# Moving a second batch from dense masked attention to gathered key blocks in a fused attention and feed-forward kernel

## The chip, the cores and the metric

The kernel runs on one core of one Trainium2 chip. The metric is device time in microseconds of one execution. A core has PE (TensorE, the matrix engine, with its weight loads shown apart as PEld), ACT (ScalarE), DVE (VectorE), POOL (GpSimd) and SP (SyncE), which here only issues transfers. Sixteen DMA engines serve all queues.

## The reference

```python
def _attn_ref(q, k, v, sampled_blocks):          # q, k, v: (4, 8, 768, 64)
    scores = scale * np.matmul(q, k.transpose(0, 1, 3, 2))
    # blocks of 32; 24 blocks; window of one block on each side; first and last block: rows and columns
    mask = np.abs(blk_i - blk_j) <= window
    mask = mask | (blk_i == 0) | (blk_j == 0) | (blk_i == n_blocks - 1) | (blk_j == n_blocks - 1)
    for qb in range(n_blocks):
        for kb in sampled_blocks[qb]:            # 3 sampled blocks for each query block
            mask[qb * block:(qb + 1) * block, kb * block:(kb + 1) * block] = True
    attn = softmax(np.where(mask, scores, -1e9))
    return np.matmul(attn, v)

def _moe_ref(x, w_in, w_out):                    # 3072 tokens, 512 -> 2048 -> 512
    r = np.maximum(x @ w_in, 0.0)
    return (r * r) @ w_out
```

The attention output of each batch, with its heads side by side, is the input of the feed-forward part. The sampled blocks come as an input, so which key blocks a query block needs is known only when the kernel runs.

## The kernel before, in words

Matmuls run in bfloat16. A unit `u` is a pair of heads of one batch; each of the four batches has four units. The feed-forward part runs on tiles T of 256 tokens, three per batch: four `hidden` groups (each four PE parts), `relu`, `square`, then `output` in eight parts, `out_copy` and `store`.

There are two ways of attention, and `SB` tells how many batches go the first way.

*Dense and masked* (batches 0 and 1 before). `scores` multiplies 256 queries with two chunks of 128 keys, `exps` takes the exponential of 1024 columns on ACT, `masks` multiplies it on DVE with a 0/1 mask `MK` (line 365), and `values` or `values_full` multiplies with V. A column of ones beside V gives the sum for `normalize`. For batch 0's first 256 queries the mask is added inside PSUM instead. `MASKED` lists the column ranges for which mask tiles are made; they lie in the buffers `VG` that the sparse batches use later.

*Gathered blocks* (batches 2 and 3 before). A visit `v` takes two pairs of query blocks, `g`. For each `g` the keys are gathered into `KG`: `k_gather` copies the window, the first and last block and the six sampled blocks out of the transposed keys of all four units, on POOL or DVE, at addresses read from registers (lines 590 to 596). V goes to DRAM by `v_store` once all four units' values are cast; `v_gather` fetches the sampled rows from there, by an indirect transfer on POOL (line 575) or by six transfers on SP, and `v_window` fetches the window and the edges. Then come `s_scores` (line 204), `s_exps` (621), `s_masks` with the small mask `MKS` (628), `s_values` (651), `s_normalize` and `s_transp`. Visit 0 has beside its one pair the query blocks at the two ends, which see all keys.

The tables for this, block numbers and `MKS`, are made by `table_load` (SP), `table_places` (POOL), `table_slots` (some 25 small DVE instructions, lines 480 to 507), `table_spread` (PE), `table_rows` and `table_masks` (DVE).

`prepare` makes each unit's loads. From unit 4 on they wait for a gate: `loads_gate` is a tiny transfer on SP that waits for a block of weights. Loads are cast to bfloat16 (`cast_qk`, `cast_v`), and q and k are transposed by DMA (`transp_dma`). Raw loads have few buffers, three for q, two each for k and v:

```python
            g = gate[GATES[min(u - HP, len(GATES) - 1)]]
...
            x = T_(transp_dma, u, w, deps=[c] + old_s, put=[qc])
```

`QKT` and `VB` hold two batches: a unit's transposes wait for the scores of the unit eight before it. A dense unit needs its own keys and queries only; a visit needs those of all four units:

```python
            kc[g] = T_(k_gather, b, v, g, get=[] if kc else [kb], deps=[ev[u][1, 0] for u in us] + ...
```

Everything is a numbered task, and `PROGRAM` is the order, written out as words: engine letter, task number and, after a slash, the PSUM buffer. Each engine runs its words strictly in this order. For loads of units that go the dense way the rows of q and k are read in runs of 1536 bytes, for the others in runs of 512 (`qn`, `kn`).

Of the kernel before, what the change touches and what calls it, by code (L numbers as in the profile page):

```python
# [13 lines left out]
BF = mybir.dt.bfloat16  # L14
# [5 lines left out]
P = 128  # L20
# [5 lines left out]
def kernel(  # L26
# [12 lines left out]
    B, H, S, D = q.shape  # L39
# [3 lines left out]
    d_model = H * D  # L43
# [17 lines left out]
    SB, VR, KG_BUFS, VG_BUFS = 2, D + 2, 2, 3  # L61
# [16 lines left out]
    MASKED = ((256, 512), (512, 768), (0, 256))  # L78
# [60 lines left out]
    RT, YS = many("r", R_BUFS, [P, TWM], F32), many("ys", YS_BUFS, [P, 2 * d_model], F32)  # L139
# [310 lines left out]
    dup, low = consts.tile([GR, SL - 4], F32, name="dup"), {}  # L450
# [22 lines left out]
    def table_slots(e):  # L473
        tmp = RT[tb["tmp"][0].at]
# [4 lines left out]
        low[0] = RT[tb["tmp"][1].at][0:D].bitcast(BF)[:, 0:5 * P].rearrange("g (s c) -> g s c", c=P)  # L479
# [301 lines left out]
    def T_(f, *args, **kw):  # L781
        return Task((lambda e: f(*args, e)), **kw)
# [146 lines left out]
    tb, mk_claims, mk_buf = {}, [], {}  # L929
# [34 lines left out]
    for T in TILES:  # L964
# [36 lines left out]
        V109 V153 V207 V332 V18 V19 V20 V28 V42 V53 V294 V29 A32 V35 P30/0 P36/1 P0/2 P33/3 V31 V37 A1 P11/0 V34 P100/1 G46 A101  # L1001
        P47/0 P104/2 V43 A105 P44/3 P102/1 V45 V57 V48 P58/2 A103 V54 P111/3 V59 P55/0 P113/2 A112 V56 P115/1 V41 P4/0 A114 G64 P9/0
        P125/3 P2/0 A116 G52 P106/2 V3 V67 A126 P5/0 P123/1 V107 G74 P65/0 A124 P108 V66 P121/3 V110 G63 P68/0 A122 P82/2 V69 P84/1
        V83 P131/0 A85 P135/2 A132 G49 P86/3 P117/1 V87 G60 A136 P88/0 P10/3 V118 P133/3 G73 A89 P61/2 P119 G38 A134 V62 P12/0 G75
        V120 P90/0 P168/2 P15/1 V91 A169 P39/1 P174/3 G78 V40 P127/0 G76 A175 P137/1 V128 G70 P144/2 V138 P129 P147/3 A145 V130 P139
        V176 P71/0 A148 V140 P171/2 V170 P781/1 P782 V72 A172 V146 P92/3 P187/0 P783 V93 A188 P784 V173 P50/2 P181/3 A785 P177/0
        V189 V51 A182 P141/1 G786 V178 P774/2 P775 A142 V149 P184/3 P179 P776 G79 G22 V180 A185 P94/1 P777 V143 P155/0 A95 V778 G787
        P150/3 A156 P158/1 V151 P161/2 A159 P788/0 V183 P152 P789 S80 V186 A154 P215/1 A162 P790 V157 P14/3 P791 V160 A216 P98/3
        P190/2 V163 A99 P212/1 S251 V792 A780 P164/3 S252 A213 V191 P795/0 G793 A779 V165 P796 S81 P209/1 G794 P192 P166 P797 V167
        V193 P798 A210 P824/3 V217 V214 S259 S260 V383 G77 P825 A799 P197/2 P194/1 P826 A198 G801 P827 P818/0 A195 V828 P819 G254  # L1010
        P226/2 A800 P820 S255 V196 A227 P200/1 P812/3 V264 P813 A201 V211 S267 P243/2 P821 V256 S265 P814 A244 V228 P218/1 P815 V199
        A822 P219 P802/2 A816 V220 S257 V202 P240/0 P221 P803 A241 V262 S261 P96/3 P804 A222 V97 A817 P237/0 V242 P223/1 P203/3 A238
        S268 V245 P805 S263 V272 A224 P229/0 P204 P806 A230 G266 S275 S276 P286/1 V225 A823 P807 S273 V231 A287 P808 V205 P232/0
        A829 V270 P206 P289/1 S271 P233 V239 V208 P809 A290 V234 V288 P296/3 S253 A810 P246/1 V291 S437 P235 P247 V236 A297 P299/2
        V248 P830/0 P831 A300 V280 P302/3 V278 P832 A303 P249 S279 P283/2 V250 P833 V298 A284 P852/1 V834 V434 P314/3 S277 P853 A315
        S281 P846/2 V304 P847 A835 V285 P311/0 P854 V258 P855 A312 V301 P848 S269 P849 V316 A856 P292/3 S21 V313 P864/0 A850 P293
        P305/1 G282 V295 P865 A857 P308/2 G851 S454 P306 S436 A309 P866 V307 P353/3 P867 A354 P326/1 V868 P858/2 G439 P859 A327
        P320/3 P860 V274 A321 P323/0 S438 V310 P836/1 S444 A324 V355 S460 P861 V322 P347/3 S445 P837 V496 A862 V328 V325 G441 P317/0
        A348 P350/2 P318 P838 S811 V319 A351 V349 P329/3 A869 P334/0 V352 P330 P839 V331 A335 V23 P356/2 G443 A863 P340/3 P840 S333
        A341 P841 P362/0 P357 G447 P842 A363 P337/3 P843 S452 A338 G459 S442 P870/0 G449 A844 P359/3 P871 S446 A360 V345 V342 V358  # L1020
        S440 V339 P374/1 P872 A375 V336 P365/2 S450 P377/3 V361 P873 A366 V364 P343/1 S462 A378 V367 P371/2 P344 S845 P874 A372 S448
        V346 V376 P368/3 P398/1 V373 P369 A399 P875 V379 S461 V370 P380/2 V470 S453 P401/1 P381 A402 P385/3 V382 P876 V400 A386 S384
        P391/2 P16/1 P877 V451 A392 V403 P404/1 P886/3 V878 A405 P887 P388/2 P425/0 A389 V406 P24/1 P888 V27 V25 A426 P889 P880/2
        A890 P881 G463 P428/0 P882 A429 G467 P883 V427 V26 S613 P407/3 G465 S631 A884 P408 S468 S469 A891 G455 S464 V396 V409 P926/0
# [64 lines left out]
```

## Time and profile before

| | |
|---|---|
| median of 3 runs | 260.05 us (257.1 to 262.1) |
| profiled execution | 257.99 us |
| its span, first to last instruction | 256.1 us |
| mean granted TensorE clock | 0.991 |
| PE, ACT, DVE, POOL busy | 95%, 72%, 65%, 38% of the span |
| DMA | 47.08 MB, mean 184 GB/s |

The span is what the engines' rows cover; the profiled time is 1.9 us longer. In a row of the windows the first number is the length of the stretch, then come busy microseconds and instruction counts (x) of each engine, the granted clock, the mean busy share of the DMA engines and GB/s. The DMA share adds queues that overlap, so it can pass 1. In a row of the timeline stand the start, the length, the engine, the line, the operation, output and inputs, the shape and the count. In a row of groups stand count, busy time in all, mean nanoseconds of one, and the idle time ahead of them with what ended it.

### The profile page before, as it was taken

To read this page: it belongs to the slowest core of one execution; us is meant where nothing else is said; L and a number is where in the kernel's file an instruction comes from. 1 tells how busy PE (TensorE), PEld (TensorE's weight loads), DVE (VectorE), ACT (ScalarE), POOL (GpSimd) and SP (SyncE) were. 2 spreads that over 40 slices of the span, in tenths; PEclk is the share of its full clock that TensorE was granted. 3 is DMA by queue.
4 is the path that set the end of the run, shared out by engine and by line. 5 is a ranking of instruction groups with operands and counts; after the bars stand their busy time and mean duration, and the time that the engine had idled before them with its cause. 6 is when DMAs were issued, how large, how long until landed. Compare 5 with 4: busy or idle time off the path is not lost.

```text
span 256.1 us, 12046 instructions
## 1 busy us (share of the span) xinstructions
PE 243.1 (95%) x5265; PEld 182.3 (71%) x5265; DVE 166.4 (65%) x386; ACT 184.5 (72%) x217; POOL 98.0 (38%) x199
## 2 busy tenths in 40 slices
PE   7699999999999998999999987999999999999995
PEld 4577889679865677886757854766975775776774
DVE  7578997789789889865446925646466478543300
ACT  3899999999998798965867662778697646325241
POOL 2175533010544033566737951062428406151030
PEclk9999999999999999999999997999999999999999
DMA  6999999999799998999999998951525554343022
GB/s 182 368 266 196 196 241 217 270 209 254 211 316 200 206 196 256 127 276 187 289 241 165 213 197 204 303 148 34 153 50 87 150 159 112 96 119 91 3 84 84
DMA packets 63540, 47.08 MB, mean 184 GB/s; under 512 B 31487, under 2 KB 58496, under 8 KB 63488
## 3 DMA queue, kind: packets, MB, share of 16 engines
q1 hardware_dynamic: 58352, 37.61, 66.7%
q0 software_dynamic: 4448, 8.25, 15.7%
q8 instruction: 41, 0.67, 1.1%
q10 hardware_dynamic: 688, 0.46, 0.6%
q14 instruction: 11, 0.09, 0.1%
HBM read 35.51 MB, written 7.91 MB: 170 GB/s over the span
## 4 chain that ended last, share of the span: by engine, by line
PE 88%; DMA 4%; DVE 2%; issue 1%; ACT 1%; another core or an unknown queue 1%; SPq 1%; DVEq 0%; ACTq 0%
PE X L204 80%; PE X L651 5%; DMA ks<-in_k_dram 2%; DMA xT<-XS 2%; PE X L396 2%; ACT pT L358 1%; PE X L306 1%; DVE ys L124 1%; DVE qc L124 0%; SPq L170 0%; PE X L425 0%; DVE QKT L124 0%; DVE pT L365 0%; DVE VB L124 0%
## 5 line engine op out<-in xcount | busy, mean ns | idle before, releaser
L204 PE MATMUL X<-xT,w_in_sb 64*128 64x256 bf16 x1536 | 99.8, 270 | 4.5 <-remote 2.5
L204 PE MATMUL X<-w_out_sb,g 64*128 64x512 bf16 (+3 forms) x960 | 95.8, 336 | 0.0
L204 PEld LDWEIGHTS <-w_in_sb 64*128 64x128 bf16 x1536 | 74.7, 94 | 16.6 <-remote 3.0
L358 ACT ACTIVATE pT<-X 128x1024 bf16<-128x1024 f32 x72 | 70.7, 1032 | 7.3 <-PE X L204 5.5
L621 ACT ACTIVATE pT<-X 128x768 bf16<-128x768 f32 (+1 forms) x56 | 41.7, 765 | 29.5 <-PE X L204 27.8
L204 PEld LDWEIGHTS <-g 64*128 64x128 bf16 x960 | 40.8, 95 | 26.7 <-issue 1.4
L716 ACT ACTIVATE g<-r 128x1024 bf16<-128x1024 f32 (+1 forms) x44 | 40.2, 929 | 11.8 <-DVE r L707 11.7
L707 DVE TENSOR_SCALAR r<-X 128x1024 f32<-128x1024 f32 x22 | 26.9, 1224 | 26.3 <-PE X L204 24.8
L365 DVE TENSOR_TENSOR pT<-pT,VG 128x1024 bf16<-128x1024 bf16 x60 | 41.0, 719 | 2.0 <-ACT pT L358 1.3
L718 POOL TENSOR_TENSOR g<-r 128x512 bf16<-128x512 f32 (+1 forms) x16 | 20.7, 1307 | 48.4 <-ACT r L705 24.8
L628 DVE TENSOR_TENSOR pT<-pT,MKS 128x768 bf16<-128x768 bf16 (+1 forms) x48 | 28.8, 631 | 13.1 <-ACT pT L621 12.7
L705 ACT ACTIVATE r<-X 128x1024 f32<-128x1024 f32 x26 | 27.3, 1063 | 9.7 <-PE X L204 8.1
L204 PE MATMUL X<-QKT 64*128 64x256 bf16 (+1 forms) x384 | 32.1, 250 | 0.7 <-issue 0.4
L575 POOL DMA_INDIRECT VG<-rows,idx x20 | 20.1, 1004 | 26.0 <-PE X L651 12.0
L204 PEld LDWEIGHTS <-QKT 64*128 64x128 bf16 x384 | 17.4, 95 | 6.4 <-issue 1.9
L204 PEld LDWEIGHTS <-pT 64*128 64x128 bf16 x768 | 15.5, 94 | 2.8 <-PE X L204 0.2
L124 POOL CAST VB<-vs 128x768 bf16<-128x768 f32 x10 | 8.5, 855 | 23.5 <-DMA vs<-in_v_dram 21.9
L204 PEld LDWEIGHTS <-KG 64*128 64x128 bf16 x528 | 13.9, 96 | 4.9 <-issue 1.0
L204 PE MATMUL X<-VB,pT 64*128 64x65 bf16 x768 | 17.2, 190 | 0.1
L124 POOL CAST qc<-ks 128x384 bf16<-128x384 f32 (+1 forms) x17 | 8.5, 530 | 21.0 <-DMA ks<-in_k_dram 16.0
L204 PE MATMUL X<-QKT,KG 64*128 64x64 bf16 x528 | 15.5, 191 | 0.3 <-issue 0.3
L596 POOL COPY KG<-QKT 128x64 int32 x72 | 14.8, 251 | 0.0
(104 smaller groups left out, 198.3 us busy)
## 6 DMA issues: line engine op xcount, KB each, us to landing
vs<-in_v_dram SPq DMA_DIRECT2D x14, 384.0 KB
ks<-in_k_dram SPq DMA_DIRECT2D x13, 384.0 KB
qs<-in_q_dram SPq DMA_DIRECT2D x12, 384.0 KB
out_dram<-ys SPq DMA_DIRECT2D x9, 512.0 KB
VG<-rows SPq DMA_DIRECT2D x20, 132.0 KB
w_in_sb<-in_moe_w_in_dram POOLq DMA_DIRECT2D x2, 1024.0 KB
w_out_sb<-in_moe_w_out_dram POOLq DMA_DIRECT2D x4, 512.0 KB, 11.0
rows<-VB SPq DMA_DIRECT2D x4, 396.0 KB
```

The costliest lines, as they stand in the source:

```text
L124: (V if e == "DVE" else G).tensor_copy(out=out, in_=in_)
L204: last = nc.tensor.matmul(out(r ^ crossed), lhsT(r ^ crossed, rows), rhs(r ^ crossed, rows), skip_group_check=True, **kw)
L358: A.activation(out=pT[:, :, 0:n], in_=stile.pop(a)[:, :, 0:n], func=AF.Exp, scale=scale)
L365: V.tensor_tensor(out=pT, in0=pT, in1=m[:, None].broadcast_to([P, 2, len(cs), w]), op=AOP.mult)
L575: G.indirect_dma_start(out=to[0:RS * HB], out_offset=None, in_=pairs, in_offset=bass.IndirectOffsetOnAxis(ap=idx[0:RS * HB, g - 1:g], axis=0))
L596: eng.tensor_copy(out=rows[:, :, :, r_ * w:(r_ + 1) * w], in_=src[:, :, :, bass.ds(at[r_] * w, w)])
L621: A.activation(out=pT[:, :, 0:n], in_=stile.pop((u, v, gs))[:, :, 0:n], func=AF.Exp, scale=scale)
L628: V.tensor_tensor(out=pT, in0=pT, in1=m[:, None].broadcast_to([P, 2, n]), op=AOP.mult)
L705: A.activation(out=to, in_=src, func=AF.Relu)
L707: V.tensor_scalar(out=to, in0=src, scalar1=0.0, scalar2=None, op0=AOP.max)
L716: A.activation(out=g, in_=r, func=AF.Square)
L718: (G if e == "POOL" else V).tensor_mul(out=g, in0=r, in1=r)
```

## The change

`SB` goes from 2 to 1, so batch 1 takes the gathered way: its loads are read in the layout of batches 2 and 3, its dense scores, masks and values go, and it gets `v_store`, `v_window`, `v_gather`, `k_gather` and six visits of its own. The mask tiles for columns 0 to 256 served batch 1 alone and go. `table_slots` works in one YS buffer rather than in two r buffers, and the tables are made in the first quarter of the program, since the first visit now comes before batch 0's feed-forward part is done. The numbers of the tasks and all orders are new.

```diff
-    SB, VR, KG_BUFS, VG_BUFS = 2, D + 2, 2, 3
+    SB, VR, KG_BUFS, VG_BUFS = 1, D + 2, 2, 3
...
-    MASKED = ((256, 512), (512, 768), (0, 256))
+    MASKED = ((256, 512), (512, 768))
...
     def table_slots(e):
-        tmp = RT[tb["tmp"][0].at]
+        tmp, spread_ = YS[tb["tmp"].at][:, 0:d_model], YS[tb["tmp"].at][:, d_model:2 * d_model]
...
-        low[0] = RT[tb["tmp"][1].at][0:D].bitcast(BF)[:, 0:5 * P].rearrange("g (s c) -> g s c", c=P)
+        low[0] = spread_[0:D].bitcast(BF)[:, 0:5 * P].rearrange("g (s c) -> g s c", c=P)
...
-    tmp = tb["tmp"] = [Buf("r"), Buf("r")]
-    tb["slots"] = T_(table_slots, deps=[t, p], get=tmp)
+    tmp = tb["tmp"] = Buf("ys")
+    tb["slots"] = T_(table_slots, deps=[t, p], get=[tmp])
...
-    t = T_(table_spread, hb, deps=[tb["slots"]], get=[hb], put=tmp)
+    t = T_(table_spread, hb, deps=[tb["slots"]], get=[hb], put=[tmp])
```

In the new `PROGRAM` the parts that the prediction speaks of stand like this. The order of the weight loads on POOL was blocks 0, 1, 4, 2, 5, 3 and is 0, 1, 4, 3, 2, 5. SP issues the first gate, unit 4's q, the tables and unit 4's v, the second gate, then k of 4 and 5, q of 7 and 6, v of 5, transposes of 4, and so on until both `v_store` of batch 1, in front of the last transposes of units 6 and 5. The tables' DVE work:

```text
before:  ... V331 A335 V23 P356/2 G443 A863 P340/3 P840 S333 A341 P841 P362/0 P357 ...
after:   ... V184 P159 P205/0 S246 P773 A160 V204 A206 P208/2 P774 P185 P775 A209 V22 P219/0 S80 A186 ...
```

(V23 before and V22 after are `table_slots`.) The three last parts of the output of tile (2, 0) stood ahead of the first visit of batch 3 on PE and stand behind it now; the other PE work behind that visit is the same.

More of the change, by code (lines that the diff above doesn't have):

```diff
@@ L1005 @@
[L1005 to L1012, printed above, removed]
@@ new lines @@
+        A942 P973 G982 V603 A577 P974 S582 P951 V975 P570/3 P965/0 S602 A571 V578 P966 G563 P573/2 P514/3 A574 G609 P967 V539 S592
+        G589 P952 S538 P968 P953 G587 S610 V515 S604 P567/2 P954 A568 V572 V575 S517 A969 V569 P551/3 P955 A976 G970 P959/2 P960
+        A552 P545/0 P956 A546 S600 G540 V553 P554/3 V957 A555 G619 S606 S588 P961 S542 P962 G541 P579/0 V559 A963 P548/3 V644
+        P1011/1 V580 A964 P999/2 P1000 G611 A597 P1005/0 P1001 A549 G648 P1002 P1012 V605 S614 A1003 V556 P632/3 P1006 S615 P1013
@@ L1057 @@
+        P1183 P1184 P1195 S1170 P1196 P1197 P1198 P1185 P1186 V1199 P1187 P1188 S1200 A1189 S1190
     """
```

97 lines of the change are left out of this document (49 added, 48 removed).

## The prediction

> **What bounds the kernel now.** I read the page's busy times and its chain first, then the windows by stage, then PE's timeline, then the DMA view by stretch.
>
> ```profile
> PE 243.1 (95%) x5265; PEld 182.3 (71%) x5265; DVE 166.4 (65%) x386; ACT 184.5 (72%) x217; POOL 98.0 (38%) x199
> PE 88%; DMA 4%; DVE 2%; issue 1%; ACT 1%; another core or an unknown queue 1%; SPq 1%; DVEq 0%; ACTq 0%
> ```
>
> By this PE bounds nearly everything. The windows (PE, PEld, DVE, ACT, POOL busy us, clock, DMA share, GB/s) say more:
>
> ```profile
> 10.00:37.00 27.00, 26.02 (x559) 21.75 (x556) 23.15 (x51) 26.16 (x32) 13.92 (x27) 1.00 1.12 243
> 37.00:64.00 27.00, 26.98 (x614) 22.58 (x611) 22.68 (x44) 26.41 (x30) 4.31 (x5) 1.00 1.11 234
> 64.00:97.00 33.00, 32.47 (x751) 22.82 (x743) 28.77 (x72) 30.23 (x33) 12.22 (x17) 1.00 1.08 222
> 97.00:120.00 23.00, 22.25 (x533) 18.23 (x534) 17.09 (x45) 17.98 (x23) 11.36 (x35) 1.00 1.13 218
> 120.00:143.00 23.00, 21.84 (x500) 16.12 (x495) 13.14 (x26) 15.83 (x19) 15.61 (x42) 1.00 1.13 220
> 143.00:166.00 23.00, 20.48 (x415) 14.82 (x410) 13.21 (x33) 12.74 (x15) 8.27 (x9) 0.93 1.12 235
> 166.00:180.00 14.00, 14.00 (x307) 9.47 (x302) 7.01 (x29) 11.44 (x15) 6.33 (x18) 1.00 0.38 95
> ```
>
> Two things besides PE are full. ACT works 97% of the time until 64 us. And the DMA share stands at 1.08 to 1.13 in every stretch until 166 us, then falls to 0.38: the DMA engines work without a break until the last batch is in, and only then does PE run alone. The chain shows what PE did around that point:
>
> ```profile
> 92.22 5.40 DMA xT<-XS
> ...
> 118.63 1.64 PE X L651 x67
> ...
> 152.51 2.47 another core or an unknown queue
> ...
> 179.28 1.64 PE X L651 x69
> ```
>
> The 1.64 us pieces are the first visits of batches 2 and 3 (`s_values` with v = 0). So batch 3's values were in by 166 plus the gather behind them, and PE wanted them at 179.3. A gather takes some 6 us from POOL's start to landing, by a row of the DMA view from 105 to 165 us:
>
> ```profile
> DMA  9199999999999999999929999999979939987989
> q1 hardware_dynamic: 19981, 10.76, 99.5%
> q0 software_dynamic: 704, 2.23, 13.8%
> VG<-rows,idx POOLq DMA_INDIRECT x11, 5.7
> ```
>
> So the data was ready at about 166 + 6 = 172, and DMA is only some 7 us behind PE as the bound. That is the slack on which this change must live.
>
> **The change: what PE saves.** Rows of PE's timeline; the step from one start to the next is what a task costs:
>
> ```profile
> 85.55 0.53 PE L204 MATMUL X<-VB,pT 64*128 64x65 bf16 x24
> 85.91 0.38 PE L204 MATMUL X<-QKT 64*128 64x256 bf16 x4
> 86.14 0.54 PE L204 MATMUL X<-VB,pT 64*128 64x65 bf16 x24
> 86.51 1.03 PE L204 MATMUL X<-w_out_sb,g 64*128 64x512 bf16 x8
> 87.38 0.53 PE L204 MATMUL X<-VB,pT 64*128 64x65 bf16 x24
> ...
> 207.50 0.95 PE L651 MATMUL X<-VG,pT 128*64 128x65 bf16 x48
> 208.39 0.35 PE L204 MATMUL X<-QKT,KG 64*128 64x64 bf16 x12
> 208.57 1.03 PE L204 MATMUL X<-w_out_sb,g 64*128 64x512 bf16 x8
> ```
>
> Dense batch 1 is 36 score tasks at 0.23 = 8.3 us and 24 half `values` at 0.365 = 8.8; three mask tiles for columns 0 to 256, six matmuls of the same width, add 0.3. Together 17.4 us. Sparse it is 24 score tasks of twelve matmuls at 0.18 and 4 of six at 0.09 = 4.7, five `s_values` at 0.89 and one at 1.64 = 6.1; together 10.8. **PE saves 6.6 us** of 256; skipping two thirds of the blocks saves little, because short matmuls cost more per column.
>
> **ACT, DVE, POOL.**
>
> ```profile
> L358 ACT ACTIVATE pT<-X 128x1024 bf16<-128x1024 f32 x72 | 70.7, 1032 | 7.3 <-PE X L204 5.5 <-ACT g L716 0.6 <-PE X L425 0.5
> L365 DVE TENSOR_TENSOR pT<-pT,VG 128x1024 bf16<-128x1024 bf16 x60 | 41.0, 719 | 2.0 <-ACT pT L358 1.3 <-ACT r L705 0.6
> L621 ACT ACTIVATE pT<-X 128x768 bf16<-128x768 f32 x48 | 38.0, 811 | 26.8 <-PE X L204 25.2 <-DVE KG L596 1.1
> L628 DVE TENSOR_TENSOR pT<-pT,MKS 128x768 bf16<-128x768 bf16 x40 | 25.6, 670 | 10.6 <-ACT pT L621 10.2 <-issue 0.4
> L596 POOL COPY KG<-QKT 128x64 int32 x72 | 14.8, 251 | 0.0
> L575 POOL DMA_INDIRECT VG<-rows,idx x20 | 20.1, 1004 | 26.0 <-PE X L651 12.0 <-DVE XS L411 7.0 <-issue 3.8
> ```
>
> ACT loses 36 x 1.03 = 37 us and gets 20 x 0.81 plus eight smaller, about 20: 17 us less. DVE loses 26 us of masks and gets 13 plus small ones plus five of the eleven key gathers: about even. POOL gets six key gathers (six copies of 0.25 and a longer one, about 2 each) and eleven issues of 1.0: 23 us more, on an engine idle 60% of the time. None of these is priced by itself: PE hid them, as its rows of 27.00 and 33.00 us show (98 to 100% busy).
>
> **The tables, moved from 75 us to about 40.** They are one piece of DVE work, between these rows:
>
> ```profile
> 74.46 0.20 DVE L480 COPY tab<-sb_r 1x72 int32<-1x72 int32 x1
> ...
> 80.54 0.16 DVE L507 TENSOR_TENSOR lane<-lane,half 128x1 f32<-128x1 f32 x1
> ```
>
> That is 6.2 us. In the new DVE order `table_slots` stands among the masks of batch 0's last columns, and behind it wait the masks of (1, 512) and (2, 512), for them ACT's exps when the eight pT buffers are full, and then PE. Between the words around it PE has only about 3.7 us of its own (five scores, two hidden parts, two output parts). In the old place it had over 6. I take 3 us of stall, bounds 0 and 6. The YS buffer that it borrows holds a v load of the start, cast long before, and the first output copy comes later: no cost.
>
> **Batch 1 must be whole.** Before, batch 1's first scores needed unit 4 alone; now `k_gather` needs the keys of all four units and `s_values` their values through DRAM. SP's and POOL's rows bound when they can start:
>
> ```profile
> 28.30 0.80 POOL L332 DMA_DIRECT2D w_out_sb<-in_moe_w_out_dram  x1
> ...
> 31.66 0.25 SPq L336 DMA_DIRECT2D scratch<-w_out_sb  x1
> 37.88 0.24 SPq L336 DMA_DIRECT2D scratch<-w_out_sb  x1
> ```
>
> The two gates wait for weight blocks 4 and 5. Block 5 now comes after 4, 3 and 2 rather than after 4 and 2, so I put the second gate 3 us later, near 41 us (a block every 3 us: 31.66, 37.88 for two more). From there SP has 10 loads, 8 transposes of 1.2 us or more and two `v_store` to issue, with the casts of the two ks buffers between: the last key transpose lands at about 62, the first `k_gather` ends near 65. Summed by such steps the new PE order has 48 us of work ahead of that point; the same sum over the old order stands 10.5 us behind the clock at 40 us; with the 3 above PE comes at 62. **2 to 3 us of stall**, bounds 0 and 7.
>
> **What DMA gets.** Batch 1 gains what batches 2 and 3 have, half of these rows of the page:
>
> ```profile
> VG<-rows SPq DMA_DIRECT2D x20, 132.0 KB
> rows<-VB SPq DMA_DIRECT2D x4, 396.0 KB
> VG<-rows SPq DMA_DIRECT2D x16, 66.0 KB
> VG<-rows SPq DMA_DIRECT2D x12, 33.0 KB
> ```
>
> Stores 2 x 396 KB, windows 10 x 132 and 2 x 66, edges 6 x 66, and eleven gathers of 6 x 33 = 198 KB: 4.8 MiB with all, 4.93 MB. At the 224 GB/s that the stretches between 64 and 166 average, 22 us. The q and k loads of batch 1 are cut into 512-byte runs like batches 2 and 3; 3.1 MB at 222 rather than at 243 GB/s, another 1 us. Nothing is taken away: transposes, weights and the four output stores ahead of batch 3's `v_store` stay. So DMA gets 23 us more ahead of the end of its full stretch. What it can take up in its pauses: the row of 40 digits has 7 to 8% of them empty, which over the 130 us until 166 is 10 us (bounds 4 and 15).
>
> The row for q0 bears on whether gathers on POOL's queue are free: with 13.8% there q1 had 99.5%, and the sum stays at the same 1.13. The Trainium skill (DMA: Bandwidth & Descriptors, Issuing engines are not separate DMA queues) says the same, that DMAs of all issuing engines run on the same 16 engines; if it were not so, the gathers' 8 us would be free and the sum below 256. By the row I count them in full.
>
> **The sum.** Batch 3's data in at 166 + 23 - 10 = 179, gathered at 185. What PE has left from its first visit: before, 256.1 - 179.3 = 76.8; the new PE order differs there by three output parts of (2, 0), 0.87 each by the rows above, that come after it now: 79.4. End at 264; but PE saves 6.6 and may fill waiting time with work placed later, and on PE's side alone the end is 256.1 - 6.6 + 3 + 2.5 = 255. Both need not meet at the worst: I take the DMA side less 2 us for work that PE may do in between, **262.4 of span**, and with the 1.9 us between span (256.1) and the profiled time (257.99) **264 us**. The median of the runs is 260.05, 2 above the profiled one; I leave that inside the range. The forecast is a little slower, 1.5%, where about 2% can be told from no change.
>
> **Rivals.**
> 1. *DMA has more room than I allow.* For it: the pauses; and that nothing in the rows shows PE waiting long for a load (5.4 us for xT is the worst). Then PE's side holds, 255 of span, 257 us, perhaps 258 with the median. Against: the flat 1.08 to 1.13.
> 2. *PE's saving comes through whole*, with tables and first gather hidden by ACT's 17 us: 249.5 of span, 251.5 us: faster. For it: PE 95% and the chain's 88%. Against: the slack of 7 us against 23.
> 3. *Slower by far: DMA takes nothing up in pauses.* The place is batch 3's `v_store`; it decides from the point at which the added transfers pass 7 us. Then 166 + 23 + 6 + 79.4 = 274 of span; with half the pauses 269, 271 us. For it: the 152.5 piece and the clock of 0.93 there show that PE already stalls and slows in this stretch. Against: PE and DMA wait for each other, so not all gaps are DMA's own.
>
> **How the numbers follow.** Forecast (259 to 268) 0.36; rival 1 (254 to 260) 0.22; rival 2 (under 254) 0.17; rival 3 (over 268) 0.25. The range 251 to 274 leaves out a tenth on either side. Faster by over 2% (under 255): rival 2 and a little of rival 1, 0.20. Slower by over 2% (over 265): rival 3 and under half of the forecast, 0.40. Within: 0.40.
>
> **What would show it.** Right: a DMA share near 1.1 until 172 to 182 us instead of 166; the last piece of 1.64 us near 183; more PE idle in the 60s and between 100 and 175; ACT at 80% and less after 50 us; POOL over 115 us busy. Wrong: a share that falls already at 166, or PE without gaps, means that the pauses were enough. If PE waits more than 7 us near 60 us for the first key gather, the early chain was mis-sized, not DMA as a whole.

## The result, and the profile after

| | before | after |
|---|---|---|
| median of 3 runs | 260.05 us | 282.46 us (280.56 to 284.2) |
| profiled execution | 257.99 us | 280.56 us |
| its span | 256.1 us | 278.8 us |
| mean granted TensorE clock | 0.991 | 0.98 |
| ratio after to before | | 1.092 (1.070 to 1.115) |

The kernel is 9% slower, 22.4 us by the medians and 22.7 by the spans. The forecast was 264, its range 251 to 274, so the time lies outside it; the nearest case was rival 3 (274 of span). On two other chips the same two kernels stood at 1.131 and 1.118, so an experiment is compared with the changed kernel of its own chip wherever that ran there, and a difference across chips is weak evidence. A few executions were disturbed: medians count all of them, ratios only the undisturbed ones, and of a profile from a disturbed one only stages up to 97 us are read.

The page of the changed kernel, busy times and the chain of work that ended last:

```profile
PE 242.3 (87%) x5163; PEld 178.0 (64%) x5163; DVE 177.5 (64%) x402; ACT 162.5 (58%) x199; POOL 126.1 (45%) x267
PE 50%; DMA 14%; issue 5%; POOL 3%; SPq 3%; ACT 1%; DVE 1%; POOLq 1%; DVEq 0%; ACTq 0%
```

PE is hardly less busy, 242.3 instead of 243.1, and idle 36.5 us (278.8 - 242.3) instead of 13.0. **All 22.7 us are idle time of PE**: 23.5 more idle, 0.8 less busy. The windows by stage tell where (columns as in the prediction):

```profile
10.00:37.00 27.00, 22.45 (x468) 17.31 (x462) 19.08 (x43) 22.65 (x26) 13.41 (x26) 1.00 1.13 236
37.00:64.00 27.00, 20.91 (x356) 16.08 (x357) 19.61 (x53) 20.17 (x27) 11.15 (x17) 0.98 1.03 231
64.00:97.00 33.00, 26.75 (x627) 20.01 (x622) 21.09 (x56) 21.14 (x28) 17.80 (x43) 0.91 1.15 222
97.00:166.00 69.00, 64.02 (x1490) 47.49 (x1490) 52.33 (x114) 42.52 (x53) 42.36 (x95) 1.00 1.03 220
166.00:180.00 14.00, 12.99 (x309) 9.70 (x306) 8.34 (x14) 9.59 (x12) 10.18 (x19) 1.00 1.24 233
180.00:200.00 20.00, 16.26 (x356) 11.46 (x350) 9.81 (x31) 10.94 (x15) 9.07 (x23) 0.91 0.97 190
```

The same of the kernel before, for the one stage that is not in the prediction:

```profile
166.00:200.00 34.00, 34.00 (x764) 24.42 (x760) 18.08 (x56) 27.46 (x34) 16.73 (x38) 1.00 0.43 96
```

Length less PE's busy time gives PE's idle time:

| stage, us | before | after | more |
|---|---|---|---|
| 10 to 37 | 0.98 | 4.55 | 3.6 |
| 37 to 64 | 0.02 | 6.09 | 6.1 |
| 64 to 97 | 0.53 | 6.25 | 5.7 |
| 97 to 166 | 4.43 | 4.98 | 0.5 |
| 166 to 200 | 0 | 4.76 | 4.8 |
| the rest | 7.0 | 9.9 | 2.8 |

So the front up to 97 us, which the forecast gave 5.5 us, loses 15.4, almost three times as much, and the middle, where it expected the DMA engines to hold PE up, nearly nothing more; then comes one wait at batch 3's first visit. The chain and PE's timeline name the waits (a timeline row ends with the idle time before it and what ended that):

```profile
57.12 6.73 DMA QKT<-qc
...
67.67 6.62 DMA QKT<-qc
74.44 6.98 PE X L204 x144
81.42 1.54 PE X L651 x67
82.96 2.10 issue
...
90.58 2.32 issue
...
137.66 1.64 PE X L651 x67
...
169.74 0.82 ACT pT L621
...
171.21 1.19 SPq L313
...
172.52 1.20 SPq L664
...
173.82 4.63 DMA vs<-in_v_dram
...
179.68 7.10 DMA rows<-VB
...
188.34 6.07 DMA VG<-rows
194.45 1.85 PE X L651 x66
```

```profile
61.75 0.66 PE L204 MATMUL X<-QKT 64*128 64x256 bf16 x8 [2.53 <-ACT pT L358]
...
74.44 0.36 PE L204 MATMUL X<-QKT 64*128 64x64 bf16 x12 [0.87 <-DMA QKT<-qc]
...
194.45 0.22 PE L651 MATMUL X<-VG,pT 128*64 128x65 bf16 x1 [3.21 <-DMA VG<-rows]
```

The three first visits stand at 81.4, 137.7 and 194.4 us. Ahead of the first the chain goes through transposes of batch 1 on SP's queue; the scores of 74.44 wait for the last two queries. Ahead of the third it goes from a visit of batch 2 (the exponentials at 169.74) over two transposes on SP to the load of V behind them, and then down the whole path of V: load, cast, store to DRAM, window, visit.

Before 64 us PE's own waits are for other engines, not for a transfer. From 10 to 37 us they are for casts, copies and exponentials on DVE, POOL and ACT; from 37 to 64 us the two largest sums are these (in all, times, longest):

```profile
PE X L204 <- ACT pT L358: 3.3, 3, 2.5
PE X L204 <- ACT r L705: 2.2, 2, 1.1
```

PE's only direct wait for batch 1's transposes up to 97 us is the 0.87 us at 74.44. So two chains arrive at that point at nearly the same time: batch 1's transposes, and PE's own work, late by its waits for the other engines.

### The profile page after: what moved, and what is told of

It is laid out like the page before. It is cut to its first block, busy times and chain, and to the rows that moved or that the text cites. A ratio compares the mean times of both kernels' runs of the same rounds, so it can differ in the third digit from the quotient of the medians.

```text
span 278.8 us, 12098 instructions
## 1 busy us (share of the span) xinstructions
PE 242.3 (87%) x5163; PEld 178.0 (64%) x5163; DVE 177.5 (64%) x402; ACT 162.5 (58%) x199; POOL 126.1 (45%) x267
## 4 chain that ended last, share of the span: by engine, by line
PE 50%; DMA 14%; issue 5%; POOL 3%; SPq 3%; ACT 1%; DVE 1%; POOLq 1%; DVEq 0%; ACTq 0%
PE X L204 44%; PE X L651 6%; DMA QKT<-qc 5%; DMA rows<-VB 3%; DMA VG<-rows,idx 2%; DMA VG<-rows 2%; DMA vs<-in_v_dram 2%; POOL g L718 1%; SPq L578 1%; POOL KG L596 1%; DMA xT<-XS 1%; SPq L664 1%; POOL qc L124 1%; ACT pT L621 1%; DVE r L707 0%
## 5 line engine op out<-in xcount | busy, mean ns | idle before, releaser
L621 ACT ACTIVATE pT<-X 128x768 bf16<-128x768 f32 (+1 forms) x84 | 62.5, 765 | 56.7 <-PE X L204 55.0
L628 DVE TENSOR_TENSOR pT<-pT,MKS 128x768 bf16<-128x768 bf16 (+1 forms) x72 | 40.8, 602 | 11.2 <-ACT pT L621 8.9
L358 ACT ACTIVATE pT<-X 128x1024 bf16<-128x1024 f32 x36 | 35.5, 1039 | 7.1 <-PE X L204 5.4
L716 ACT ACTIVATE g<-r 128x1024 bf16<-128x1024 f32 (+1 forms) x27 | 24.9, 929 | 11.6 <-DVE r L707 11.5
L590 POOL COPY KG<-QKT 128x256 int32<-128x256 int32 x20 | 10.3, 515 | 37.8 <-PE X L204 27.7
L596 POOL COPY KG<-QKT 128x64 int32 x120 | 27.1, 274 | 0.0
L204 PE MATMUL X<-QKT 64*128 64x256 bf16 (+1 forms) x288 | 19.2, 230 | 7.7 <-ACT pT L358 3.1
L651 PEld LDWEIGHTS <-pT 128*64 128x64 bf16 x936 | 18.0, 111 | 12.3 <-issue 7.7
L651 PE MATMUL X<-VG,pT 128*64 128x65 bf16 x792 | 19.2, 197 | 5.5 <-DMA VG<-rows 3.6
L365 DVE TENSOR_TENSOR pT<-pT,VG 128x1024 bf16<-128x1024 bf16 x24 | 17.5, 762 | 7.5 <-ACT pT L358 6.3
```

Of the source, the lines that this page charges most:

```text
L204: last = nc.tensor.matmul(out(r ^ crossed), lhsT(r ^ crossed, rows), rhs(r ^ crossed, rows), skip_group_check=True, **kw)
L358: A.activation(out=pT[:, :, 0:n], in_=stile.pop(a)[:, :, 0:n], func=AF.Exp, scale=scale)
L365: V.tensor_tensor(out=pT, in0=pT, in1=m[:, None].broadcast_to([P, 2, len(cs), w]), op=AOP.mult)
L596: eng.tensor_copy(out=rows[:, :, :, r_ * w:(r_ + 1) * w], in_=src[:, :, :, bass.ds(at[r_] * w, w)])
L621: A.activation(out=pT[:, :, 0:n], in_=stile.pop((u, v, gs))[:, :, 0:n], func=AF.Exp, scale=scale)
L628: V.tensor_tensor(out=pT, in0=pT, in1=m[:, None].broadcast_to([P, 2, n]), op=AOP.mult)
```

## The experiments

The theories that the expectations speak of: the DMA side as the prediction has it (theory 1: what V costs on its way through DRAM holds PE up); the front (theory 2: batch 1's keys and queries come late, and V is worth only part); the tables (theory 3); the new order, which loses small waits everywhere (theory 4); and later, SP's queue, on which loads, transposes, stores and windows go strictly in order (theory 6). PE's lag is the time on the clock less the work that PE has done by then.

### The path of V

**v_unread.** `s_values` of batch 1 reads the dense values instead of what came back from DRAM; the transfers stay.

```diff
+ if g == 0 or b == SB: val = VB[...]
```

> The changed kernel, but batch 1's s_values reads batch 1's V where it lies (VB) instead of the gathered blocks; all its transfers are issued as before, nobody waits for them (the attention of batch 1 is then not the reference's). Amount of DMA (theory 1: the 22 us of transfers that batch 1 gained make the loss): the same transfers, so no change, 281 to 283 us. Batch 1 must be whole (theory 2: its loads, casts and transposes are through DMA only near 74 us): no change either, since the keys decide, not V; 280 to 283. Tables (theory 3) and order (theory 4: the new order loses small waits everywhere): no change. If V's way through DRAM (store, then gather, some 13 us) were what the visits of batch 1 wait for, 272 to 276.

283.13 us, ratio 1.102 (1.093 to 1.110): no gain over the 282.46 of the changed kernel, which ran on another chip. In the trace of after too PE has no wait ahead of batch 1's first visit at 81.4: that visit does not wait for V's data.

**v_left_out.** As v_unread, and batch 1's `v_store`, `v_window` and `v_gather` return at once, so 4.9 MB don't move.

```diff
+ if b == SB: return          # v_store, v_window, v_gather
```

> As v_unread, but batch 1's v_store, v_window and v_gather are not issued at all: 4.9 MB less. Theory 1 (amount): some 18 of the 22 us come back, 262 to 266 us, and the DMA share falls near 176 instead of 200. Theory 2 (whole batch 1): the lag of PE until 74 us stays, since the transfers left out come after it; what comes back is from 74 on, 6 to 9 us, 273 to 276. Theories 3 and 4 (tables, order): 281 to 283.

275.11 us, ratio 1.070 (1.057 to 1.083), 8 us under v_unread on the same chip. That is the 6 to 9 of theory 2 and not the 18 of theory 1. Its window:

```profile
64.00:97.00 33.00, 28.20 (x711) 19.95 (x712) 24.32 (x69) 22.91 (x31) 12.89 (x44) 0.95 0.68 142
```

The DMA share falls from 1.15 to 0.68, PE's idle time there only from 6.25 to 4.8. Batch 1's first visit stays at 80.6 (81.4 in after).

**before_plus_v.** The converse: to the kernel before are added the store, windows and rows of batch 1's V, written to DRAM buffers that nobody reads.

```diff
+ def x_window(v, e): ... sy.dma_start(out=dump(...), in_=<rows of batch 1>)     # line 1009, 1011
+ def x_rows(i, e): ...                                                          # on POOL's queue
```

> The kernel before with the transfers that batch 1 gains in the change, and nothing else of it: its V is stored (2 x 396 KB) near 70 us, and windows, edges and 11 gathers of 198 KB go from there to memory that nobody reads, spread between 80 and 125 us on SP and POOL. Theory 1, as in the prediction's sum: 22 us of DMA, 10 of them in pauses, 7 of slack, so 5 to 6 us over before: 261 to 263 where before is at 256. No pauses taken up (the prediction's third rival): 12 to 15 us, 268 to 271. If DMA had room: 256 to 258.

270.93 us, ratio 1.049 (1.041 to 1.056): 12.4 us, the value that was expected if the pauses take up nothing. The trace says by what. PE has one long wait and the chain ahead of it shows SP's queue at work:

```profile
104.36 1.89 PE L204 MATMUL X<-xT,w_in_sb 64*128 64x256 bf16 x16 [7.03 <-DMA xT<-XS]
```

```profile
97.31 1.14 SPq L1009
...
99.12 0.59 SPq L1011
...
100.45 1.22 SPq L438
...
101.72 2.50 DMA xT<-XS
```

In the kernel before this transpose goes out at 89.2 us, and PE has no wait of 2 us or more up to 120 us. The transpose of the attention's output (line 438), on which the feed-forward part waits, stands on SP behind a transpose, loads and the added windows. Batch 3's first visit comes at 189.5 (before 179.3); by the prediction's way of counting, 166 + 22 + 6 = 194 with nothing taken up, so that some 5 us were taken up and not 10. One wait of 7.0 us is most of the 10.9 us by which the span is longer: the added transfers cost by their place on a queue as well as by their length.

**v_load_first.** The changed kernel with one word of SP's order moved: the last load of V (unit 14) to a place right behind `G589`, ahead of `S538`.

```diff
- ... S538 ... S600 ...
+ ... S600 S538 ...
```

> The changed kernel with one word of SP moved: the last v load of batch 3 (unit 14) is issued right behind that of unit 13, instead of behind two transposes of x and two of q and k that wait for PE's visits of batch 2. If SP's in-order queue ties batch 3's data to PE's progress (theory 6: PE, SP and DMA wait for each other in a loop): v_store, windows and the first visit of batch 3 come 3 to 5 us earlier, the wait of 3.6 us at that visit goes, and the end is 3 us earlier, 0.01 of the ratio. If DMA's bytes decide (theory 1): v lands no earlier than DMA gets to it, 0 to 1 us.

279.21 us, ratio 1.087 (1.067 to 1.106). SP is through with that load at 169.8 instead of 175.1 us; nothing else was moved, so words ahead of it on SP had held it back. The wait of 3.21 us at batch 3's first visit is gone, and the span is 276.2, 2.6 less than after's on another chip; the interval is too wide to show so small a step in the time. But the wait can't be put down to the load: `v_store`, which follows it, goes out no earlier (179.5, in after 179.1), and the wait is gone as well in tables_short and k_unread, where SP's order is as in the change.

### The front

**tables_short.** `table_slots` does seven of its instructions.

```diff
- <some 18 more DVE instructions of table_slots>
+ copy tab; memset(low, 1.0); copy ids; spread(4, ids); half, lane
```

> The changed kernel with table_slots cut from some 29 instructions on DVE to 9 (the block numbers are still made, the small mask comes out as ones, so attention counts doubled blocks twice). The piece on DVE falls from 7.0 to about 2 us. Theory 3 (tables): 5 us of the loss come back, 276 to 278 us. Theory 2 (whole batch 1): PE waits for the transposes near 74 us all the same, 281 to 283. Theory 1 (amount): 281 to 283.

277.99 us (277.71 to 286.09), ratio 1.085 (1.076 to 1.093). The time alone would be theory 3's. The trace is against it: the tables' piece ran in after from

```profile
40.65 0.18 DVE L480 COPY tab<-sb_r 1x72 int32<-1x72 int32 x1
...
47.45 0.34 DVE L507 TENSOR_TENSOR lane<-lane,half 128x1 f32<-128x1 f32 x1
```

and without most of it the stage is

```profile
37.00:64.00 27.00, 20.82 (x361) 15.91 (x358) 15.96 (x34) 20.24 (x28) 11.90 (x16) 1.00 1.03 233
```

PE 20.82 busy instead of 20.91, batch 1's first visit at 81.4 in both. The 3 us for the tables were 0 on PE in this stage. Beside v_unread, on the same chip, the run is 5.1 us faster; from 10 to 97 us PE idles 1.4 us more than there, and what it gains lies behind (166 to 200 us: 1.8 us idle instead of 5.1). What made it so is not settled.

**w_out_once.** Weight block 2, the first of the four of `w_out`, serves for all of the output. The loads of blocks 3, 4 and 5 go, both gates wait for block 2, and the second opens at about 34 us instead of 41. The output is then not the reference's.

```diff
+ if i > NWI: return                       # w_load
- w_out_sb[rows, f, ...]
+ w_out_sb[rows, f % (NF // NWO), ...]
```

> The changed kernel with only the first of the four blocks of w_out loaded and used for all four (the feed-forward output is not the reference's), and both gates behind this block: three transfers of 3.1 us of DMA less ahead of batch 1's loads, which start near 31 us instead of 41. Theory 2 (whole batch 1, DMA full in front of it): the restart of PE at 74.4 us comes 8 to 10 us earlier and the end with it, 271 to 274 us. Theory 1 (amount): 9 us less of DMA also counts, but at the end: PE's lag at 74 us stays and the end falls to 273 to 276. Theories 3 and 4: the lag by 45 us and the waits of the order stay, 279 to 283.

278.29 us, ratio 1.082 (1.071 to 1.092), 5 us under v_unread on the same chip, where 8 to 10 us were expected to go. The first loads behind the gate come 7 us earlier (34.5), the last of the keys not at all (49.2, in after 49.1), and the first visit 3 (78.4). POOL shows why:

```profile
46.34 1.04 POOL L721 TENSOR_TENSOR g<-r 128x512 bf16<-128x512 f32 x1 [6.33 <-ACT r L708]
47.32 1.88 POOL L124 CAST qc<-ks 128x384 bf16<-128x384 f32 x2
```

POOL has casts of batch 1's keys behind a `square` that waits 6.3 us for ACT's `relu`. With earlier loads it is the order of the engines that holds the casts back.

**front_37.** The changed kernel with the old order of some 200 words at the start on every engine but SP, up to the first `hidden` word of tile (0, 256). That includes the old order of the weight blocks on POOL, 0, 1, 4, 2, 5, 3.

```diff
- PROGRAM = <new order> 
+ PROGRAM = <old order of PE, ACT, DVE, POOL to 37 us> + <new order without these words>
```

> The changed kernel with the front of the old order: up to the old order's first hidden part of tile (0, 256), 37.9 us in the profile of before, every engine but SP takes batch 0's work (and the weight loads, blocks 0, 1, 4, 2, 5, then 3) as in the kernel before; then the new order goes on with what is left. Theory 4 (the new order loses small waits): PE's lag behind its own work at 46 us falls from 17 to 11 or 12 us, and some 4 of these 5 us reach the end, 275 to 278. Theory 2 (batch 1's loads, casts and transposes decide the restart at 74 us): the lag falls at 46 us but is back at 24 or 25 by 75, 279 to 282. A weight order that lets the second gate open some 4 us earlier goes with it; by theory 2 that gives at most 3 us.

290.31 us, ratio 1.112 (1.101 to 1.123); after_again on the same chip 292.78, 1.131 (1.123 to 1.139).

> The changed kernel once more, unchanged, for comparison on the chip of the next three: 1.07 to 1.11 of the kernel before, 278 to 284 us.

PE's idle time from 10 to 37 us falls to 2.9 (after_again 4.7) and that from 37 to 64 rises to 7.9 (7.2); the scores of the last queries start at 75.6 (75.5), batch 1's first visit at 85.6 (84.7). What PE gains by the old order it loses at a wait that the change does not have, for a weight block:

```profile
49.25 1.89 PE L204 MATMUL X<-w_out_sb,g 64*128 64x512 bf16 x8 [5.40 <-DMA w_out_sb<-in_moe_w_out_dram]
```

So front_37 does not price the order of the front by itself.

**front_wout.** Both, front_37 and w_out_once. Beside it the changed kernel as it is, after_third.

```diff
+ <edits of front_37 and of w_out_once>
```

> front_37 and w_out_once together (the old order's front, and only one of four w_out blocks loaded, so the feed-forward output is not the reference's). Theory 5: PE's restart near 74 us has two chains behind it that must both be in, batch 1's loads (gates) and the casts and squares that stand on POOL, ACT and DVE behind the dense front; each alone moved the restart by 0 to 3 us, so both together move it by more than the sum: PE's lag at the restart falls from 25 to 17 to 19 us, and the end is 6 to 9 us under after_third. If a third thing decides (two k and two v raw buffers, transposes of 5 us behind each other on SP): 3 us at the restart as with w_out_once alone, 3 to 4 at the end.

> The changed kernel unchanged, for comparison on the chip of the next three: 1.08 to 1.13 of the kernel before.

287.17 us against 290.86, ratios 1.090 (1.076 to 1.104) and 1.118 (1.107 to 1.128): 7 us by the ratios, inside the 6 to 9. Its stage

```profile
37.00:64.00 27.00, 22.94 (x471) 17.44 (x469) 22.41 (x60) 21.10 (x25) 14.27 (x29) 1.00 1.20 227
```

idles 4.1 us (after_third: 5.6), and the scores of the last queries start at 69.5 instead of 73.8; without the late blocks front_37's wait for weights is gone. From 64 to 97 us it idles 8.3 us instead of 6.3 and so gives back 2.0 of the 2.9 us that it gained up to 64. The two edits alone were worth 5 us each by the ratios, on other chips (w_out_once beside v_unread, front_37 beside after_again), so both together gain less than their sum, where theory 5 expected more.

**casts_pool.** Three casts of batch 1 (V of units 5 and 6, k of unit 6) go from ACT and DVE to POOL. The reason is this row of ACT in after, a cast that stands waiting for its load while the exponentials that PE waits for at 61.75 are queued behind it:

```profile
59.94 0.83 ACT L122 CAST VB<-vs 128x768 bf16<-128x768 f32 x1 [3.33 <-DMA vs<-in_v_dram]
```

```diff
- A259 A267 V263
+ G259 G267 G263
```

> The changed kernel with three casts of batch 1 (V of units 5 and 6 on ACT, k of unit 6 on DVE) given to POOL at the same places of the order. Theory 7: until 70 us PE still works on batch 0 and tile (0, 256), and loses because casts that wait for loads stand in front of exps, relus and masks on ACT and DVE: the waits of PE near 54, 62 and 69 us (1.3, 2.7 and 1.0 us) go, its lag at 69 us falls from 24 to 20, and 2 to 4 us of it reach the end. If ACT and DVE are late for other reasons (the order of batch 0's work): 23 to 24 at 69 us and no change at the end; POOL, later by some 3 us, may then put the first k_gather off, 1 to 2 us slower.

283.15 us, ratio 1.089 (1.068 to 1.110). On this chip after_third stood at 290.86 and 1.118 (1.107 to 1.128); the intervals just overlap. The front gains nothing: the wait of 2.53 us goes and the idle time from 37 to 64 us falls to 4.2, but the scores start again only when the transposes are in:

```profile
74.38 0.51 PE L204 MATMUL X<-QKT 64*128 64x64 bf16 x12 [1.97 <-DMA QKT<-qc]
```

74.38 here, 73.76 in after_third and 74.44 in after: a stall that goes ahead of a later one is paid there. From 10 to 97 us PE idles 15.8 us in casts_pool and in after_third; what separates their times lies behind that and is open. The point near 74 us is held by these rows of SP in after:

```profile
57.12 6.16 SPq L313 DMA_TRANSPOSE QKT<-qc  x2
...
64.02 2.13 SPq L313 DMA_TRANSPOSE QKT<-qc  x1
...
67.67 4.04 SPq L313 DMA_TRANSPOSE QKT<-qc  x2
```

They are not the only bound: in v_left_out, without the two stores between them, SP is through with the last transposes at 67.3 instead of 71.7, PE does not wait for them, and it starts the same scores at 72.0. Up to there it is late by its own waits.

### Does the front lose by itself?

**before_v_none, after_v_none, after_kv_none.** In the first two no gathered visit, of any batch, has V through DRAM: `s_values` reads the dense values, and stores, windows and gathers return. In the third the scores read the dense keys too, so no visit waits for `k_gather`. All three leave out that part of the computation.

```diff
+ val = VB[...]                                        # s_values, all g
+ return                                               # v_store, v_window, v_gather
+ return QK[i][rows, 1, c * P:(c + 1) * P]             # s_scores' keys, after_kv_none
```

> The kernel before with no V transfers in the gathered batches at all (2 and 3): v_store, v_window and v_gather are not issued and s_values reads V where it lies (attention of these batches is then not the reference's). 9.9 MB less, some 44 us of DMA. PE sets the end before; its lag grows from 11 to 21 us between 92 and 167, and some 5 to 8 us of that should go: 248 to 252 where before is 256 to 259.

> The same of the changed kernel, for batches 1, 2 and 3: 14.8 MB less. If V's way through DRAM were all of the loss, PE's saving of 6.6 us would show: 6 us under before_v_none, 242 to 246. If the front until 74 us loses by itself what it lost there (14 us more lag than before) and nothing makes it good: 14 less 6.6 = 8 us over before_v_none, 256 to 260. If the queues lose further in the later stages without V too (theory 6): 262 to 266.

> after_v_none, and the gathered scores read the keys where they lie too; k_gather is carried out and waited for by nobody. A visit then needs the transposes of its own unit only, as a dense unit does. If 'a batch must be whole' is the cause (theory 2): the restart near 74 us comes earlier by several us and the later stages lose little, 4 to 8 us under after_v_none. If casts, transposes and queues decide: 0 to 2 us under it.

On one chip, where the kernel before took 257.94 and the changed kernel did not run: 253.74 (ratio 0.984, 0.969 to 0.999), 263.74 (1.029, 1.016 to 1.042) and 258.61 (1.008, 1.004 to 1.012). Without any V through DRAM the new kernel is still 10.0 us slower than the old one; if the change lost by V alone, it would have been faster. The windows, old and then new:

```profile
37.00:64.00 27.00, 25.66 (x559) 20.52 (x556) 21.74 (x43) 25.51 (x29) 4.19 (x5) 1.00 1.09 224
```

```profile
10.00:37.00 27.00, 22.39 (x465) 17.25 (x459) 18.99 (x43) 22.57 (x26) 13.35 (x26) 1.00 1.14 235
37.00:64.00 27.00, 21.35 (x363) 16.31 (x363) 20.40 (x53) 20.41 (x27) 10.60 (x17) 0.98 1.05 242
64.00:97.00 33.00, 29.83 (x726) 21.48 (x724) 25.06 (x71) 24.07 (x32) 13.52 (x44) 0.91 0.67 141
166.00:200.00 34.00, 34.00 (x812) 25.80 (x810) 24.48 (x70) 25.04 (x32) 12.82 (x36) 1.00 0.34 69
```

The new order idles 4.6 and 5.7 us before 64 us, as with V (4.55 and 6.09), where before_v_none idles 1.0 and 1.3: **the front's loss up to 64 us has nothing to do with V.** From 64 to 97 us it idles 3.2 instead of 0.9, so that the whole 10 us lie ahead of 97. From 166 us PE is full, 34.00 of 34.00. The ratios price V in each order: 1.000 - 0.984 = 0.016 or 4.2 us in the old one, 1.092 - 1.029 = 0.063 or 16 us in the new one, of which batch 1's are 8 by v_left_out. So V of batches 2 and 3 alone costs some 8 in the new order and 4 in the old; the 16 and the 8 join numbers of different chips. The gathered keys are worth 263.74 - 258.61 = 5 us, for all three batches, and PE's idle time from 10 to 64 us stays at 9.6 without them, so they cost in the visits and not in the front. What they cost in the old order was not measured.

**k_unread.** As in after_kv_none, but for batch 1 alone and with V through DRAM as in the change.

```diff
+ if b == SB: return QK[i][rows, 1, c * P:(c + 1) * P]
```

> The changed kernel, but batch 1's s_scores read the keys where they lie (QKT) instead of the gathered ones; the k_gather instructions are carried out as before and nobody waits for them (batch 1's attention is then not the reference's). If the place of k_gather on POOL, behind casts and v_gather issues, is what PE waits for in batch 1: 3 us at 95 to 100 us come back and 1 to 2 elsewhere, 276 to 278. If transposes (theory 2) or DMA (theory 1) decide: 279 to 282.

289.04 us (285.38 to 290.58) against 292.78 of after_again on that chip, 3.7 us or 1.3%, with ranges that don't overlap. PE still waits for the last queries' transposes, until 76.7, and the first visit comes at 84.8 (after_again 84.7). Theory 2 in its first form, PE waiting for the first key gather, falls: that gather ends at 71.5, ahead of the queries' transposes.

### Put together

**front_wout_v** takes front_wout and leaves out batch 1's V transfers, **all_five** also reads batch 1's keys dense and shortens the tables.

```diff
+ <front_wout> + <v_left_out>
+ <front_wout> + <v_left_out> + <k_unread> + <tables_short>
```

> front_wout and v_left_out together: batch 1's V transfers aren't issued either. If the losses until 74 us and the V transfers add (one in front of the other): the sum of front_wout's gain and the 8 us of v_left_out, 14 to 17 us under after_third. If each only uncovers the other (DMA's bytes are one bound, PE's lag from the front the other, and the later wins): with both away the whole loss goes, 20 us or more under after_third, close to the kernel before.

> front_wout_v, and also batch 1's keys read where they lie (k_gather carried out, not waited for) and the small tables. What is left is the new order itself behind 74 us. By the PE sum alone (6.6 us less work than before) this kernel could end 6 us under the kernel before, 0.97 to 0.98 of it; if the new order and the later stage lose by themselves, 1.01 to 1.04.

277.43 and 274.8 us, where the kernel before took 259.58 and after_third 290.86. front_wout_v is 13.4 us under after_third, just short of the 14 to 17 that were expected if the losses add and far from the 20 or more if each only uncovers the other. all_five misses its expectation: with batch 1's V and keys, the tables, the weights' gate and the front's order taken out the new kernel is still some 15 us behind. Part of it is the 6.8 us that PE still idles from 10 to 64 us; the rest is open.

**after_mended** joins what had helped or done no harm: front_37, casts_pool and v_load_first.

```diff
+ <front_37> + <casts_pool> + <v_load_first>
```

> casts_pool, front_37 and v_load_first in one, with the whole computation: the changed kernel as the runs so far would mend it. By the lags seen: 1 to 2 us from the front, 2 to 4 from the casts, 3 from the v load, if they add; the changed kernel stood at 1.09 to 1.13 of the kernel before on three chips, so 1.06 to 1.10. It stays slower than the kernel before; under 1.04 would say that the order, not the transfers, was most of the loss.

281.71 us, ratio 1.078 (1.059 to 1.097), as expected: below after_third's 1.118 (1.107 to 1.128), casts_pool beside it 1.089. It does not beat the kernel before.

## Why the prediction was wrong

**The step that failed is the sum, and in it the term for the front.** The sum put PE's side at 255 and the DMA side at 262 and took the later of the two, since "both need not meet at the worst". The two were measured apart: the new order without any V loses 10.0 us (after_v_none less before_v_none), where the prediction gave the front 5.5 and PE a saving of 6.6; and batch 1's V added to the old order, whose front is whole, loses 12.4 (before_plus_v). The later of the two would be 12. Measured were 22.4, which is their sum. That the sum fits so closely is luck: the numbers come from three chips, and on the chip of before_plus_v the change costs 34 us. That the losses come on top of each other is borne out by two pairs of runs, each on one chip. In the new order batch 1's V is still worth 8 us (v_left_out against v_unread), where the later of 10 and 12.4 would leave it 12.4 - 10 = 2.4; and front_wout_v gains on after_third nearly what was expected if the losses add.

Why they add is argued and not shown. The later of two holds when the early loss gives the DMA engines time to get ahead. Here the loads of batches 2 and 3 are words of the same SP queue as batch 1's transposes, stores and windows, and wait for buffers that PE's scores free, so what PE loses in the front the loads can lose too. The chain of after has one such tie: the last load of V, at 173.82, stands behind two transposes that follow the exponentials of a visit of batch 2.

By its steps:

- *PE saves 6.6 us.* The steps from start to start read the same in after (0.17 to 0.18 for twelve score matmuls), but PE's busy time fell by 0.8. A task that starts behind a pause counts its whole length (0.38 where the step was 0.23), and slow clocks behind pauses add to it: by the mean clocks some 3 us more than before, an estimate (0.020 of 278.8 us against 0.009 of 256.1).
- *ACT, DVE and POOL.* ACT 184.5 to 162.5, expected 17 less; POOL 98.0 to 126.1, expected 23 more; DVE 166.4 to 177.5, expected about even. None is a bound by its share. But the forecast priced the engines by busy time, and POOL and ACT cost by position: a cast behind a waiting `square`, exponentials behind a waiting cast.
- *The tables: 3 us.* 0 on PE up to 97 us (tables_short). The piece took 7 us at 40.65 to 47.79, where forecast.
- *Batch 1 must be whole: 2 to 3 us, bounds 0 and 7.* With the tables this was all that the prediction gave the front, which lost 9.6 us more of idle time ahead of 64 us. The gate came at 40.99, as forecast; the transposes didn't. They were counted at 1.2 us and more on SP, and batch 1's eight held it 1.2 to 3.4 us each, 17.6 in all. The step ended at the last key transpose, forecast 62 and measured 68.2, and forgot the queries, whose last transposes landed at 74.3. But PE's direct wait for them was 0.87 us. The larger part is PE's waits for DVE, POOL and ACT: 3.6 us more idle up to 37 us, before the second gate opens, and 6.1 from there to 64, of which the longest wait, 2.5 us, is for exponentials behind a cast that waits for a load of batch 1. These waits the prediction put at nothing. Of the loss ahead of 64 us about two thirds stay even in front_wout (6.6 us idle, after_third 9.5, before 1.0); what holds them is open.
- *DMA gets 23 us and takes up 10 in pauses, 7 are slack.* Batch 3's first visit was forecast at 183 to 185 and came at 194.4; that rival 3's 166 + 23 + 6 = 195 names the time is luck, since its mechanism, DMA without pauses, is not what the windows show. Two figures of that step are slightly off and change nothing: 4.93 MB are 4.7 MiB, and eleven gathers of 198 KB are 10 us at 224 GB/s, not 8. From 97 to 166 the share is 1.03, not 1.12: the DMA engines had room there that they didn't use. before_plus_v says the same of the old order: 10 us later at that visit by the added transfers.
- *What PE has left from there: 79.4.* It had 278.8 - 194.4 = 84.4.
- *Rivals 1 and 2.* Both fell: the gap ahead of batch 3's first visit is there, and nothing of PE's saving came through.
- *The signs.* Share near 1.1 until 172 to 182 us: it stayed high until about 200 (0.97 from 180 to 200 us, then 0.60). ACT under 80% behind 50 us and POOL over 115 us: both so. "If PE waits more than 7 us near 60 us ... the early chain was mis-sized": it was, though the stall is spread from 10 to 97 us.

On the other two chips the change costs some 10 us more. The stage where after_third falls behind has fewer matmuls (1242 against 1490), more idle time, a lower share and clock, and a wait that no queue of the profile explains; its cause is open:

```profile
97.00:166.00 69.00, 59.61 (x1242) 41.26 (x1244) 45.20 (x100) 34.99 (x44) 35.25 (x80) 0.93 0.80 189
```

```profile
120.53 2.34 another core or an unknown queue
```

## What to carry to other kernels

Before a slack of one resource and a stall of another are compared by "the later of the two", look for what ties them; where loads, transposes and stores share one in-order queue and wait for buffers that the late engine frees, as here, the sum is the safer bound. When work is turned from "needs its own unit" to "needs all four", walk the chain of the last input of every kind (here queries, not keys) to its landing, with the queue's own time for each transfer. Price a new order by position too: a cast that waits for a load holds back whatever stands behind it on its engine. And taking one stall away tells little while the next one stands behind it: the pair of before and after, both without the suspect (here V), says more than either half.

## What the runs showed of the hardware

**The clock can drop behind short pauses.** In after PE pauses 2.5 us up to 61.75, 2.3 us up to 92.9 and 3.2 us up to 194.45, in before 2.5 us up to 155; the windows behind them:

```profile
64.00:66.00 2.00, 2.00 (x45) 1.87 (x42) 2.00 (x3) 1.77 (x2) 1.80 (x2) 0.50 0.85 174
```

```profile
93.00:97.00 4.00, 4.00 (x43) 2.06 (x41) 3.06 (x5) 2.49 (x3) 1.46 (x7) 0.57 1.48 146
```

```profile
194.40:198.00 3.60, 3.55 (x101) 2.77 (x103) 1.28 (x3) 1.23 (x2) 1.08 (x2) 0.72 1.06 275
```

```profile
155.00:158.00 3.00, 2.97 (x46) 1.84 (x48) 0.77 (x2) 1.06 (x2) 0.00 (x0) 0.64 0.90 199
```

In windows of 1 us the granted clock holds for about 1 us behind the pause and then stands at 0.50 for about 3, so that the longer windows above show 0.57 to 0.72: at 0.57 a stretch of 4 us does the work of 2.3, 1.7 us more on top of the pause. Behind the pauses of 2.1 us at 83 and of 2.4 us up to 235.1 it did not fall, so the length of a pause alone does not decide it. The Trainium skill (TensorE: Matmul & The Clock Gate, Why this matters for your kernels) asks for no gaps of PE over about 3 us; here 2.3 to 2.5 us were enough in three cases, and the measurement decides.

**PE stood twice in the middle of a task.** The pauses of 2.10 and 2.32 us at 82.96 and 90.58 have no releaser in the profile ("issue"), and at the start of each one transfer of an instruction queue (q8) was under way, while the DMA engines were full:

```profile
q1 hardware_dynamic: 1381, 0.91, 112.0%
q8 instruction: 1, 0.02, 2.5%
```

That is the DMA view of 81 to 85.1 us; 85.1 to 90 us has no such row. In v_left_out both pauses are gone; one of 1.48 us, up to 77.8, stands where the share is still 1.03, and none behind it, where the share falls to 0.32 (78 to 92 us). Against it: from 97 to 166 us, at a share of 1.03, the same queue has 11 transfers and PE no such pause. That PE waited for its instructions behind data is argued from this and not shown. The Trainium skill (Runtime: NRT & Kernel Launch, Instruction fetch mechanics) has the sequencer fetch its next block by a queue of its own at a cost that is mostly hidden; if the reading is right, the 4.4 us here are a case in which it wasn't.
